# Last rows' operands in a gated unit: four buffers of parts, their stores on GpSimd's queue, and a step between the loads of raw blocks and their use

## The chip, the cores and the metric

The kernel runs on one core of a Trainium2 chip. A core has TensorE (PE, with its weight loads shown as PEld), VectorE (DVE), ScalarE (ACT), GpSimd (POOL) and SyncE (SP), each with its own queue of instructions that it takes strictly in order; they meet only at semaphores. DMAs are issued from the queues of SP and POOL. The metric is the device time of one execution in microseconds, the median of the runs shown; the clock is the one that TensorE was granted, as a share of full speed.

## The reference, cut to what matters

A transformer block with adaptive layer norm: attention with 32 heads, then a gated unit, on 2048 rows of 576 features. The part around the change is the gated unit:

```python
h = _layernorm(x, axis=-1) * (1 + cb) + sb
g = jnp.einsum("bsd,df->bsf", h, w_gate)      # 576 -> 4608
u = jnp.einsum("bsd,df->bsf", h, w_up)        # 576 -> 4608
h = _sigmoid(g) * u
x = x + gb * jnp.einsum("bsf,fd->bsd", h, w_down)   # 4608 -> 576
```

All in float32, to float32's precision.

## The kernel before

The kernel keeps float32's precision on a faster matmul type: each operand is a sum of a rounded part and a remainder, and a product takes the three larger of the four partial products. In the gated unit it also cuts the matrix products in two by two blocks and takes seven products in place of eight (Strassen's scheme in Winograd's form): seven operands made of sums and differences of blocks of the rows, seven of the weights.

The rows are handled in two halves of 1024. For a half, the unit goes over 18 blocks of 256 hidden features; in each it runs the seven products in the order 1, 6, 2, 7, 5, 4, 3 (`ORDER`). A product is 14 matmuls (line 1027): seven for the gate, seven for the up projection. Behind products 6 and 7 stands a down projection of the block before (`down`, line 1063): 48 matmuls into eight banks in turn, of which three exist (`d`), each emptied by an addition on DVE into `Oa` (line 1067). The second half of the rows runs the same blocks, and reads its weight operands back from HBM.

In the first half every weight operand `w` is made on the chip, three products ahead (`LOOK`), into one of four buffers: POOL builds the sums S1, S2, S3 of raw weight blocks (`put`, line 875), ACT rounds (line 909), DVE takes the remainder of five sixths of it and POOL that of the last sixth, 64 partitions of it (both line 914), and SP stores it for the second half (`ws`, line 915). A product's seventh matmul is the first that reads POOL's share. SP also loads the raw weight blocks (lines 850 and 852) and the down weights (line 1047).

Beside the first half's blocks runs a generator, `last_rows`, one step at every second product. It finishes the rows of the second half: their output projection, their layer norm, six transposed blocks for each 512 rows, stored as `hs`, and at its end their operands for the seven products. For the operands it goes three times (i = 0, 1, 2: three slices of features) through the following: load four raw blocks `B` from `hs` (line 1186), then `operand_parts`: seven parts, each a copy rounded on ACT into a buffer `ho` (line 713), a remainder on POOL (line 715; for i = 2 line 720, twice for 32 partitions), and a store of `ho` to `xs` (lines 716 and 721); between them four differences of the blocks on POOL (line 724). The raw blocks lie in five buffers `B`, the parts in `ho`. The stores are read only when the second half begins.

The order on each engine is set when the program is built. A scheduler places the instructions of all steps by its own costs, except on PE, whose order is as written from the ninth block on (`manual_schedule`). So a generator's step is where its instructions are handed over, not where they run.

Of the kernel before, what the change touches and what calls it, by code (L numbers as in the profile page):

```python
# [16 lines left out]
F32R = mybir.dt.float32r  # L17
# [6 lines left out]
P = 128  # L24
# [27 lines left out]
def tile_block(ctx, tc, x_in, wqkv, wo, w_gate, w_up, w_down, c_in, w_mod, out):  # L52
    nc = tc.nc
# [94 lines left out]
    def ln_stats(pool, xt, mv):  # L148
        st = pool.tile([P, 2, nc.vector.BN_STATS_DIM], F32, name="st", bufs=2)
        for g in range(2):  # L150
            nc.vector.bn_stats(st[:, g, :], xt[:, g, :] if len(xt.shape) == 3 else xt[:, g * HALF : (g + 1) * HALF])
        nc.vector.bn_aggr(mv, st)

    def ln_scales(pool, mv, rs):
        for _ in ln_scales_steps(pool, mv, rs):
            pass
# [522 lines left out]
    def ln_rows(z, t, x1, eng):  # L679

        zx = z[:, :, 0:HALF]
        eng.tensor_scalar(
            zx, x1, mv2[:, t, 0:1], rs2[:, t : t + 1], op0=ALU.subtract, op1=ALU.mult
        )
        nc.gpsimd.tensor_copy(
            z[:, :, HALF:384].rearrange("p g (r c) -> p g r c", c=32),
            z[:, :, HALF - 32 : HALF].unsqueeze(2).to_broadcast([P, 2, 3, 32]),
        )

    def ln_spill(zs, ch, psum, pool, put):  # L690


        for g in range(2):
            for i in range(3):
                pt = psum()
                for j, z in enumerate(zs):
                    nc.tensor.transpose(pt[:, j * P : (j + 1) * P], z[:, g, i * P : (i + 1) * P], ident)
                ev = pool.tile([P, 512], F32, name="ev", bufs=2)
                c = 3 * g + i
                put(ev, pt, mcol2[:, 0, c : c + 1], mcol2[:, 1, c : c + 1])  # L700
                nc.sync.dma_start(hs[g, i, :, ch * 512 : (ch + 1) * 512], ev)
                yield

    def operand_parts(half, i, blocks, parts, hi, lo_eng, queue):

        b11, b12, b21, b22, t3 = blocks

        def put(k, t):  # L710
            s = ORDER.index(k)
            ho = parts()
            hi(ho[:, 0, :], t)
            if i < 2:
                lo_eng.tensor_sub(ho[:, 1, :], t, ho[:, 0, :].bitcast(F32))
                queue.dma_start(xs[half, s, :, i : i + 4 : 3, :].bitcast(F32), ho.bitcast(F32))
            else:
                for q in (32, 96):
                    lo = ho[q : q + 32, 0, :]
                    lo_eng.tensor_sub(lo, t[q : q + 32], lo.bitcast(F32))  # L720
                queue.dma_start(xs[half, s, :, 2, :].bitcast(F32), ho[:, 0, :].bitcast(F32))

        def sub(to, a, b):
            nc.gpsimd.tensor_tensor(to, a, b, op=ALU.subtract)

        sub(t3, b22, b12)
        put(1, b11)
        yield
        sub(b12, b12, b11)
        put(3, b22)  # L730
        yield
        sub(b22, b22, b12)
        put(2, b21)
        yield
        sub(b21, b21, b22)
        for k, t in ((6, b22), (7, t3), (5, b12), (4, b21)):
            put(k, t)
            yield
# [335 lines left out]
    blocks = {(0, 0): begun}  # L1074
# [34 lines left out]
    def last_rows():  # L1109


        def psum():
            return pd.tile([P, 512], F32, name="d")

        with tc.tile_pool(name="fin", bufs=1, side="right") as pool:
            w = pool.tile([P, 2, 2, D], F32R, name="w")
            nc.gpsimd.dma_start(w, wod)
            for t0 in (0, 4):
                od = pool.tile([P, 4, 256], F32, name="od")
                nc.sync.dma_start(od[:, :, 0:192], oend[:, t0 : t0 + 4, :])  # L1120
                nc.sync.dma_start(od[:, :, 192:256], oend[:, t0 : t0 + 4, 128:192])
                yield
                pt = psum()
                for j in range(4):
                    nc.tensor.transpose(pt[:, j * P : (j + 1) * P], od[:, j, 0:P], ident)
                oh = pool.tile([P, 512], F32R, name="oh")
                ol = pool.tile([P, 512], F32R, name="ol")
                nc.vector.tensor_copy(oh, pt)
                nc.vector.tensor_sub(ol, pt, oh.bitcast(F32))
                pt = psum()  # L1130
                for j in range(4):
                    nc.tensor.transpose(pt[:, j * P : (j + 1) * P], od[:, j, P:256], ident)
                om = pool.tile([P, 512], F32R, name="om")
                omh = pool.tile([P, 512], F32R, name="omh")
                nc.vector.tensor_copy(om[0:64], pt[0:64])
                nc.vector.tensor_copy(omh[64:P], pt[64:P])
                nc.vector.tensor_sub(om[64:P], pt[64:P], omh[64:P].bitcast(F32))
                yield
                for j in range(4):
                    rows = slice(j * P, (j + 1) * P)  # L1140
                    xt = pool.tile([P, D], F32, name="xt", bufs=2)
                    nc.sync.dma_start(xt, x1p[:, t0 + j, :])
                    for h in range(2):
                        cols = slice(h * HALF, (h + 1) * HALF)
                        acc = psum()
                        ts_ = ((oh, 0, 0), (oh, 1, 0), (ol, 0, 0), (om, 0, 1), (om, 1, 1))
                        for n, (a, i, k) in enumerate(ts_):
                            nc.tensor.matmul(
                                acc[:, :HALF], a[:, rows], w[:, i, k, cols], start=n == 0, stop=n == 4
                            )  # L1150
                        nc.vector.tensor_add(xt[:, cols], xt[:, cols], acc[:, :HALF])
                    nc.sync.dma_start(x1d[:, t0 + j, :], xt)
                    yield

        def modulated(ev, pt, scale, bias):
            nc.scalar.activation(ev, pt, AF.Identity, scale=scale, bias=bias)

        with tc.tile_pool(name="zp2", bufs=1, side="right") as zp:
            for ch in (2, 3):
                zs = []  # L1160
                for t in range(4 * ch, 4 * ch + 4):
                    z = zp.tile([P, 2, 384], F32, name="z", bufs=4)
                    x1 = z[:, :, 0:HALF]
                    for g in range(2):
                        nc.sync.dma_start(z[:, g, 0:HALF], x1d[:, t - 8, g * HALF : (g + 1) * HALF])
                    ln_stats(zp, x1, mv2[:, t, :])
                    zs.append(z)
                four = slice(4 * ch, 4 * ch + 4)
                ln_scales(zp, mv2[:, four, :], rs2[:, four])
                for j, z in enumerate(zs):  # L1170
                    ln_rows(z, 4 * ch + j, z[:, :, 0:HALF], nc.vector)
                yield
                yield from ln_spill(zs, ch, psum, zp, modulated)
        with tc.tile_pool(name="xop2", bufs=2) as pool:

            def get():
                return [pool.tile([P, 512], F32, name="B", bufs=5) for _ in range(5)]

            def parts():
                return pool.tile([P, 2, 512], F32R, name="ho")  # L1180

            for i in range(3):
                blocks = get()
                for (g, r), t in zip(((0, 0), (0, 1), (1, 0), (1, 1)), blocks):
                    cols = slice(HW + r * 512, HW + (r + 1) * 512)
                    nc.sync.dma_start(t, hs[g, i, :, cols])
                yield from operand_parts(1, i, blocks, parts, nc.scalar.copy, nc.gpsimd, nc.sync)

    def banks(*names):
        return [pg.tile([P, 512], F32, name=n, bufs=3 if n == "x" else 1) for n in names]  # L1190
# [1 line left out]
    def half(t, v):  # L1192
        return t[:, 512 * v : 512 * (v + 1)]

    rows2 = last_rows()
    before = None
    for n, (hf, b, k) in enumerate(seq):
# [84 lines left out]
```

## Time and profile before

| | us |
|---|---|
| median of 3 runs | 2952.17 (2949.37 to 2953.37) |
| the profiled execution | 2953.87 |
| its span, from the first to the last instruction | 2952.1 |

| engine | busy us | share of the span |
|---|---|---|
| PE | 2890.3 | 98% |
| PEld | 1888.9 | 64% |
| DVE | 2139.3 | 72% |
| ACT | 1614.7 | 55% |
| POOL | 813.7 | 28% |

Where the last rows' operands run (ACT's first copy into `ho` of this stage starts at 1933.66 us, its last at 2064.34 us), the profile shows:

| | us |
|---|---|
| subtractions on POOL for the operands, lines 715, 720 and 724 | 18.4, 20.2, 16.6 |
| copies on ACT, line 713, 21 of them | 13.0 |
| idle time of ACT just before these copies | 60.2 |

How to read it: a line of the profile names an engine, an operation, its output and input by the program's names, and a count; a wait names the instruction that waited and the one that released it. A share of busy time is a mean over stages with different limits; what a stage is bound by is read from its own waits. The stage of the gated unit runs from about 1660 us to the end.

### The profile page before, as it was taken

How to read it: one execution, taken by the hardware profiler on the slowest of the kernel's cores; microseconds unless marked ns; L12 is line 12 of the kernel's file. 1: busy time of each engine (PE TensorE's matmuls, PEld its weight loads, DVE VectorE, ACT ScalarE, POOL GpSimd, SP SyncE). 2: the span in 40 equal slices, each digit the busy share in tenths (PEclk: the TensorE clock that was granted, in tenths of full speed). 3: DMA queues.
4: the chain of work that ended last, by engine and by line, in shares of the span. 5: the costliest groups of instructions: out<-in, count | busy, mean ns of one | idle time of the engine just before them, and what ended most of it. 6: DMA issues, size and time to landing. Idle time of an engine off the chain costs nothing.

```text
span 2952.1 us, 46641 instructions
## 1 busy us (share of the span) xinstructions
PE 2890.3 (98%) x17141; PEld 1888.9 (64%) x17141; DVE 2139.3 (72%) x3896; ACT 1614.7 (55%) x3022; POOL 813.7 (28%) x972
## 2 busy tenths in 40 slices
PE   7999999999999999999999999998999999999999
PEld 5756333433344444444443788877888888888888
DVE  7465888888888888998883777766777555555555
ACT  3214889999999888999889323333333111111111
POOL 3102005444303111464103534467544100000000
PEclk9999999999999999999999999999999999999999
DMA  5325213333302111222214766676666845444443
GB/s 178 101 87 185 71 31 131 121 130 126 117 26 80 53 33 44 90 75 70 60 62 161 271 237 235 232 265 237 217 215 217 317 161 178 166 166 170 162 157 136
DMA packets 137261, 425.97 MB, mean 144 GB/s; under 512 B 18884, under 2 KB 56520, under 8 KB 124744
## 3 DMA queue, kind: packets, MB, share of 16 engines
q1 hardware_dynamic: 121272, 342.42, 34.2%
q0 software_dynamic: 15760, 80.56, 7.6%
q8 instruction: 135, 2.21, 0.3%
q14 instruction: 94, 0.77, 0.1%
HBM read 264.45 MB, written 157.95 MB: 143 GB/s over the span
## 4 chain that ended last, share of the span: by engine, by line
PE 90%; ACT 2%; DVE 2%; DMA 2%; POOL 2%; issue 1%; SPq 1%; POOLq 0%; DVEq 0%; ACTq 0%
PE o L533 17%; PE d L1063 14%; PE x L1027 14%; PE s L955 13%; PE s L442 11%; PE bg L1027 5%; PE bu L1027 5%; PE s L294 4%; PE s L330 2%; PE s L672 2%; ACT p L959 1%; PE s L557 1%; ACT oT L547 1%; POOL S L875 0%; DMA B<-hs 0%
## 5 line engine op out<-in xcount | busy, mean ns | idle before, releaser
L959 ACT ACTIVATE p<-s 128x512 f32<-128x512 f32 x2048 | 1068.5, 608 | 142.9 <-PE s L442 91.7
L455 DVE TENSOR_REDUCE mx<-s 128x1 f32<-128x512 f32 x1568 | 1019.6, 686 | 169.7 <-PE s L442 156.2
L442 PE MATMUL s<-k,q 54*128 54x512 f32 x1920 | 649.7, 439 | 2.1 <-ACT p L959 1.6
L955 PE MATMUL s<-q,k 56*128 56x512 f32 x1920 | 578.7, 433 | 2.6
L955 PEld LDWEIGHTS s<-q,k 56*128 56x128 f32 x1920 | 274.8, 186 | 472.8 <-ACT p L959 304.7
L533 PE MATMUL o<-p,vaug 128*32 128x512 f32 x4096 | 555.8, 608 | 0.0
L1063 PE MATMUL d<-wd,hh 128*128 128x288 f32 x2304 | 470.0, 299 | 17.7 <-DVE Oa L1067 17.1
L1063 PEld LDWEIGHTS d<-wd,hh 128*128 128x128 f32 x2304 | 379.5, 191 | 26.9 <-DVE Oa L1067 21.5
L1067 DVE TENSOR_TENSOR Oa<-Oa,d 128x288 f32<-128x288 f32 x576 | 257.7, 452 | 152.6 <-PE d L1063 149.0
L442 PEld LDWEIGHTS s<-k,q 54*128 54x128 f32 x1920 | 308.4, 185 | 69.3 <-ACT p L959 38.5
L1063 PE MATMUL d<-wd,hl 128*128 128x288 f32 x1152 | 344.0, 299 | 0.0
L1027 PE MATMUL x<-k,w 128*128 128x512 f32 x994 | 239.6, 392 | 2.2 <-DVE u L1241 2.2
L1039 ACT ACTIVATE u<-u 128x512 f32<-128x512 f32 x72 | 45.5, 632 | 328.4 <-DVE u L1229 309.7
L1063 PEld LDWEIGHTS d<-wd,hl 128*128 128x128 f32 x1152 | 219.9, 191 | 0.3 <-DVE hl L1043 0.3
L1027 PEld LDWEIGHTS x<-k,w 128*128 128x128 f32 x994 | 184.7, 188 | 39.6 <-DVE u L1241 2.9
L533 PEld LDWEIGHTS o<-p,vaug 128*32 128x32 f32 x4096 | 83.5, 108 | 164.9 <-issue 149.4
L1069 POOL DMA_DIRECT2D out_dram<-Oa x16 | 8.7, 542 | 607.5 <-DVE Oa L1067 607.5
L1036 ACT ACTIVATE sg<-x 128x512 f32<-128x512 f32 x36 | 21.5, 598 | 282.5 <-PE x L1027 282.5
L450 DVE CUSTOM_DVE_ANT_0 rise<-s,rise 128x512 f32<-128x512 f32 x240 | 163.5, 681 | 0.0
L448 ACT ACTIVATE rise<-s 128x512 f32<-128x512 f32 x240 | 151.4, 631 | 0.0
L914 POOL TENSOR_TENSOR w<-S,w 64x256 fp32r<-64x256 f32 x69 | 72.0, 1044 | 214.2 <-ACT w L909 202.5
L1027 PE MATMUL x<-w,w 128*128 128x512 f32 x504 | 121.3, 390 | 0.0
(240 smaller groups left out, 3812.8 us busy)
## 6 DMA issues: line engine op xcount, KB each, us to landing
w<-ws SPq DMA_DIRECT2D x126, 640.0 KB
ws<-w SPq DMA_DIRECT2D x124, 640.0 KB
wd<-wds SPq DMA_DIRECT2D x36, 1152.0 KB
wds<-w POOLq DMA_DIRECT2D x18, 1152.0 KB, 4.5
k<-kd SPq DMA_DIRECT2D x30, 360.0 KB
w<-in_B_w_down_dram POOLq DMA_DIRECT2D x18, 576.0 KB, 5.0
q<-qd SPq DMA_DIRECT2D x64, 144.0 KB
raw<-in_B_w_gate_dram SPq DMA_DIRECT2D x34, 256.0 KB
```

The source lines that it names most:

```text
L294: nc.tensor.matmul(acc, w, hT[:, t, cols], start=n == 0, stop=n == len(ts_) - 1)
L442: nc.tensor.matmul(sp, qs[rows, qt * P : (qt + 1) * P], ks[rows, kc * 512 : (kc + 1) * 512], start=True, stop=True,)
L448: nc.scalar.activation(rise, sp, AF.Relu)
L450: nc.vector.tensor_tensor_reduce(rise, sp, rise, 1.0, -3.0e38, ALU.add, ALU.max, mx[0][:, qt, 0:1])
L455: nc.vector.tensor_reduce(mx[h][:, qt, j : j + 1], sp, axis=AX.X, op=ALU.max)
L533: nc.tensor.matmul(acc[32 * j : 32 * j + 32, :], vaug[:, kt, (2 * p + h) * VW : (2 * p + h) * VW + 32], probs[2 * c + h], start=kt == 0, s ...
L914: eng.tensor_sub(w[rows, :, to, :], src[rows, :, a, :], w[rows, :, a, :].bitcast(F32))
L955: nc.tensor.matmul(sT, ks[rows, kcols], qs[rows, c * 512 : (c + 1) * 512], start=True, stop=True)
L959: state["exp"] = nc.scalar.activation(pr, sT, AF.Exp, scale=SCALE)
L1027: nc.tensor.matmul(acc[v], w[:, v, a, :], X[s][:, b, :], start=first and n == 0, stop=n == 6, skip_group_check=not first,)
L1063: nc.tensor.matmul(acc[:, :HALF], a[:, f, rows], w[:, f, cols], start=n == 0, stop=n == 5)
L1067: nc.vector.tensor_add(Oa[:, t, cols], Oa[:, t, cols], acc[:, :HALF])
```

## The change

The parts get a pool of four buffers instead of two; the generator takes a step between the loads of raw blocks and the first part made of them; and the stores of the parts are issued from POOL's queue instead of SP's.

```diff
             def parts():
-                return pool.tile([P, 2, 512], F32R, name="ho")
+                return pool.tile([P, 2, 512], F32R, name="ho", bufs=4)
 
             for i in range(3):
                 blocks = get()
                 for (g, r), t in zip(((0, 0), (0, 1), (1, 0), (1, 1)), blocks):
                     cols = slice(HW + r * 512, HW + (r + 1) * 512)
                     nc.sync.dma_start(t, hs[g, i, :, cols])
-                yield from operand_parts(1, i, blocks, parts, nc.scalar.copy, nc.gpsimd, nc.sync)
+                yield
+                yield from operand_parts(1, i, blocks, parts, nc.scalar.copy, nc.gpsimd, nc.gpsimd)
```

No instruction of PE moves. ACT, POOL and SP get another order from the point on at which the operands begin. On POOL, before the change, from the third set's first part to POOL's share of the weights for the second product of the fourth block with operands, `w<-S_24925` (`w<-` are POOL's shares of weight operands, `ho<-B` remainders of parts, `B<-B` differences of blocks):

```order
L720 TENSOR_TENSOR ho<-B,ho 32x512 x2
L914 TENSOR_TENSOR w<-S_24576,w 64x2x128
L875 TENSOR_TENSOR S_24925<-S_24924,raw_24585 128x384 x2
L724 TENSOR_TENSOR B<-B 128x512
L914 TENSOR_TENSOR w<-raw_24585,w 64x2x128
L724 TENSOR_TENSOR B<-B 128x512
L720 TENSOR_TENSOR ho<-B,ho 32x512 x2
L724 TENSOR_TENSOR B<-B 128x512
L720 TENSOR_TENSOR ho<-B,ho 32x512 x2
L724 TENSOR_TENSOR B<-B 128x512
L914 TENSOR_TENSOR w<-S_24925,w 64x2x128
```

And with the change, the last rows ahead of POOL's share of the weights for the second product of that third block, `w<-S_24572`:

```order
L914 TENSOR_TENSOR w<-raw_24236,w 64x2x128
L721 DMA xs<-ho 128x512
L724 TENSOR_TENSOR B<-B 128x512
L720 TENSOR_TENSOR ho<-B,ho 32x512 x3
L721 DMA xs<-ho 128x512
L720 TENSOR_TENSOR ho<-B,ho 32x512 x2
L721 DMA xs<-ho 128x512
L720 TENSOR_TENSOR ho<-B,ho 32x512 x2
L721 DMA xs<-ho 128x512
L720 TENSOR_TENSOR ho<-B,ho 32x512
L721 DMA xs<-ho 128x512
L914 TENSOR_TENSOR w<-S_24572,w 64x2x128
```

All parts of the third set and all 21 stores now stand ahead of this weight operand of the third block; before, the same row of the fourth block still had four of the third set's parts behind it.

On SP, with the change, the third set's second, third and fourth raw blocks (`B<-hs`; `raw` are weight blocks, `ws` stores of weight operands):

```order
L1186 DMA B<-hs 128x512
L915 DMA ws<-w 128x1280
L1186 DMA B<-hs 128x512
L915 DMA ws<-w 128x1280
L850 DMA raw_24643<-in_B_w_gate_dram 128x2x256
L852 DMA raw_24643<-in_B_w_gate_dram 128x1x256
L850 DMA raw_24643<-in_B_w_up_dram 128x2x256
L852 DMA raw_24643<-in_B_w_up_dram 128x1x256
L1186 DMA B<-hs 128x512
L915 DMA ws<-w 128x1280 x2
```

Before the change these three loads stood together in one row, behind a store of a part:

```order
L716 DMA xs<-ho 128x2x512
L1186 DMA B<-hs 128x512 x3
L915 DMA ws<-w 128x1280
L721 DMA xs<-ho 128x512
L915 DMA ws<-w 128x1280
```

The stores of parts have left SP's queue, and between the loads of a set now stand stores and loads of the weights.

## The prediction

> **What bounds the kernel now.** I read the busy line first, then the waits of the gated unit, then TensorE block by block around the last rows' operands, and at last the queues of ACT and POOL there. PE is busy for 98% of the span (the page's first part), so only its gaps can be won or lost. In the gated unit a block of the hidden dimension is seven products and two down projections, and its first product is the one that reads `X[0]`. Cut at these first products (us, then the busy time of PE, PEld, DVE, ACT and POOL, the granted clock, the DMA share and GB/s), the blocks on and behind the last rows' operands stand thus:
>
> ```profile
> 1924.90:1966.50 41.60, 38.22 (x198) 33.82 (x197) 24.78 (x41) 15.28 (x24) 29.51 (x25) 0.92 0.79 272
> 1966.50:2008.40 41.90, 37.26 (x196) 32.70 (x195) 26.40 (x42) 13.95 (x22) 27.88 (x25) 0.96 0.71 236
> 2008.40:2051.40 43.00, 38.26 (x195) 33.91 (x194) 26.36 (x40) 14.76 (x23) 30.11 (x26) 0.92 0.78 270
> 2051.40:2092.80 41.40, 37.44 (x196) 32.26 (x195) 31.32 (x44) 14.07 (x22) 31.35 (x27) 0.96 0.60 218
> 2092.80:2127.80 35.00, 35.00 (x196) 31.11 (x195) 25.70 (x42) 11.42 (x18) 16.90 (x16) 1.00 0.63 217
> ```
>
> I call the first three blocks A, B and C. An undisturbed block takes 35.00 us, so the four blocks with operands lose 41.60 + 41.90 + 43.00 + 41.40 - 4 x 35.00 = **27.9 us**. That is all the change can win; POOL's busy time in them (28 to 31 us, against 16.9) is what it can run into. Who waits for whom there (1925 to 2080 us: total, times, longest):
>
> ```profile
> ACT ho L713 <- DMA xs<-ho: 35.9, 11, 7.2
> ACT ho L713 <- DMA B<-hs: 18.6, 5, 6.5
> PE d L1063 <- DVE Oa L1067: 14.4, 5, 4.7
> DVE w L914 <- ACT w L909: 8.3, 7, 5.0
> PE x L1027 <- DVE u L1241: 2.2, 1, 2.2
> ```
>
> One of the stalls, engine by engine (start, duration, instruction, idle time before it and its releaser):
>
> ```profile
> 1989.84 0.62 ACT L713 CAST ho<-B 128x512 fp32r<-128x512 f32 x1 [5.21 <-DMA B<-hs]
> 1992.60 1.02 DVE L914 TENSOR_TENSOR w<-raw,w 128x512 fp32r<-128x512 f32 x1 [4.97 <-ACT w L909]
> 1994.04 0.63 PE L1063 MATMUL d<-wd,hh 128*128 128x288 f32 x2 [4.51 <-DVE Oa L1067]
> ```
>
> ACT stands at a cast of an operand, the weights' cast stands behind it on ACT, the weights' remainder waits on DVE, the additions that empty PE's banks stand behind that, and PE stops. PE idles 14.4 + 2.2 = 16.6 us in this way; the other 11 us of the 27.9 are matmuls at a lower granted clock behind each stop (0.92 and 0.96 above). The price of one stop shows in one product, whose halves stand ahead of a stop and behind it:
>
> ```profile
> 2051.42 1.75 PE L1027 MATMUL x<-k,w 128*128 128x512 f32 x7
> 2055.34 3.02 PE L1027 MATMUL x<-k,w 128*128 128x512 f32 x7 [2.17 <-DVE u L1241]
> ```
>
> That is 1.3 us for seven matmuls and some 2 us until the clock is back.
>
> **The change part by part.** *Four buffers of parts* end waits of ACT for a store two parts earlier, 35.9 us of ACT's time. *Stores on POOL's queue* take 21 issues off SP, each 0.43 us in the median, and put them on POOL (min/median/max in ns, as POOL issues the same tiles for the first rows):
>
> ```profile
> L716 SPq DMA_DIRECT2D xs<-ho x14: 370/426/1247, 1937.0 to 2028.8; - x14
> L716 POOL DMA_DIRECT2D xs<-ho x5: 725/725/792, 1229.0 to 1301.9; - x5
> L721 POOL DMA_DIRECT2D xs<-t x5: 540/560/631, 1323.6 to 1359.2; - x5
> 1238.90 0.72 POOL L716 DMA_DIRECT2D xs<-ho  x1 [0.30 <-POOL ho L715]
> ```
>
> 14 x 0.73 + 7 x 0.56 = 14.1 us, and 0.30 more where the store stands right behind the subtraction that fills it. SP computes nothing; POOL makes a sixth of every weight operand and the sums S1 to S3. (The Trainium skill, "DMA: Bandwidth & Descriptors", section "Issuing engines are not separate DMA queues", says that transfers from all queues share the same 16 DMA engines and that another issuing engine saves only sequencer time; by that the stores land no sooner and the saving is SP's 9 us, which PE waits for in no row above. It speaks against this part and leaves the sum as it is.)
>
> *Blocks a turn ahead.* The order shows the first set's loads where they were, so the wait of 4 us for them stays. Those of the second and third sets come earlier in SP's queue, but into buffers that POOL still reads.
>
> *What the new order does* outweighs all three. The fences of the section on the change show it: nothing holds the parts back on ACT, so the order now packs all 21 into blocks A and B, where they were spread over four. POOL runs strictly in this order, and between the weights of A's sixth product and those of C's second (`w<-S_24572`) now stand 40 operand subtractions, 21 DMA issues, 10 sums and, with that last one, 10 weight operands. The price of each (busy us, mean ns, 1925 to 2080 us):
>
> ```profile
> L720 POOL TENSOR_TENSOR ho<-B,ho 32x512 fp32r<-32x512 f32 x14 | 20.2, 1444 | 1.6 <-ACT ho L713 0.7
> L715 POOL TENSOR_TENSOR ho<-B,ho 128x512 fp32r<-128x512 f32 x14 | 18.4, 1317 | 14.1 <-ACT ho L713 13.8
> L724 POOL TENSOR_TENSOR B<-B 128x512 f32<-128x512 f32 x12 | 16.6, 1380 | 7.5 <-DMA B<-hs 6.8
> L914 POOL TENSOR_TENSOR w<-S,w 64x256 fp32r<-64x256 f32 x15 | 15.0, 999 | 12.1 <-issue 7.1 <-ACT w L909 3.8 <-POOL ho L715 0.5
> L914 POOL TENSOR_TENSOR w<-raw,w 64x256 fp32r<-64x256 f32 x11 | 9.4, 857 | 0.9
> L875 POOL TENSOR_TENSOR S<-raw 128x384 f32<-128x384 f32 x8 | 10.0, 1268 | 2.9 <-DVE w L914 2.8
> L875 POOL TENSOR_TENSOR S<-raw,raw 128x384 f32<-128x384 f32 x8 | 9.1, 1153 | 0.3
> ```
>
> Subtractions 20.2 + 18.4 + 16.6 = 55.2; weights 10 x 0.94 (24.4 over 26) = 9.4; sums 10 x 1.2 (between the two rows) = 12.0; issues 14.1: **90.7 us of work in one queue.** It starts and is due here:
>
> ```profile
> 1935.72 1.29 POOL L715 TENSOR_TENSOR ho<-B,ho 128x512 fp32r<-128x512 f32 x1
> 1938.38 2.66 POOL L724 TENSOR_TENSOR B<-B 128x512 f32<-128x512 f32 x2 [1.37 <-DMA B<-hs]
> 1924.90 3.47 PE L1027 MATMUL x<-k,w 128*128 128x512 f32 x14
> 1928.21 1.75 PE L1027 MATMUL bg<-k,w 128*128 128x512 f32 x7
> ```
>
> The queue is done no earlier than 1935.7 + 90.7 = 2026.4. To this come its waits: 0.3 for the first loads (most of the 1.37 is now filled by the first issue), 0.3 at each of four stores right behind their subtraction (1.2), about 2 for A's fifth product, whose end frees a weight buffer, with DVE's remainder behind it, and about 4 for the third set's fourth block. That block's load stands on SP behind a load that waits for POOL's last part of the second set, then a store, a load, a store and four raw loads: some 4 us of issue, and then the landing:
>
> ```profile
> 1975.97 0.42 SPq L1186 DMA_DIRECT2D B<-hs  x1
> 1980.45 0.62 ACT L713 CAST ho<-B 128x512 fp32r<-128x512 f32 x1 [6.52 <-DMA B<-hs]
> ```
>
> 4.5 us here; so 8.5 or more, while POOL has two stores, two subtractions and a third store left, 5 us. Together 7.5: **2033.9**. Undisturbed, PE is at C's second product at 1924.9 + 2 x 35.0 + 3.3 = 1998.2, and at its seventh matmul, the first that reads POOL's part of the weights, 1.4 us later, 1999.6. So blocks A to C lose 2033.9 - 1999.6 = 34.3 us, and the slow clock behind this last stop 2 more: 36.3. Behind it POOL has two sums and one weight instruction until the next product that could wait, with a down projection between, and no operands are left, so I count nothing further. The net is 36.3 - 27.9 = **+8.4 us**. The ACT path ends near the same point: four casts stand ahead of the sigmoid of B's `u3` and wait for POOL's last subtractions, so it adds little on top.
>
> The two ends: with the operand subtractions at 1.28, weights at 0.86, sums at 1.15 and no waits, 51.2 + 8.6 + 11.5 + 14.1 = 85.4, done at 2021.1, a loss of 21.5, or -6.4 us net. That is a floor, since the order is fixed. At the other end POOL and DVE slow each other when both work without a break:
>
> ```profile
> 2041.72 2.63 POOL L720 TENSOR_TENSOR ho<-B,ho 32x512 fp32r<-32x512 f32 x2
> 2055.35 6.89 POOL L720 TENSOR_TENSOR ho<-B,ho 32x512 fp32r<-32x512 f32 x4
> 2057.60 1.78 DVE L914 TENSOR_TENSOR w<-S,w 128x512 fp32r<-128x512 f32 x1
> ```
>
> 1.72 us each instead of 1.32. With 40 at 1.72 the queue has 68.8 instead of 55.2, +13.6, or +22 net. (The Trainium skill's "GPSIMD Engine Reference", section "1. Specifications", says that POOL shares its SBUF interfaces with VectorE, in contention above all with instructions of two SBUF inputs, as this weight remainder is; a fuller POOL queue would then meet more of them, towards the upper end. The trace agrees as far as 6.89 us for four.)
>
> **The rivals.** *POOL bound, but with no more loss than now* (no change): its work runs near the floor with few waits, 25 to 30 us lost, 2949 to 2956 us. For it speaks that DVE idles while PE stands, which makes POOL quicker; against it the four named waits. *The stores were the fault* (faster): only the stops that follow an ACT wait for a store go away, about half of the 27.9, so 2952.2 - 14 = 2938 us. For it speak the 35.9 us of ACT; it decides only if POOL's queue reaches C's second weights some 14 us after 1999.6, while the floor is 2021.1. *Contention* (slower still): the 22 us above, 2974 us. *The loads are not ahead* where it matters: true of the first set, and part of my sum; were the third set's wait of 4 us gone, 2956.6.
>
> **How the numbers follow.** The profiled execution took 2953.87 us with a span of 2952.1, 1.7 above the median of the runs; from the median 2952.17 + 8.4 = **2960.6 us**. Chances: POOL's queue as summed 0.60, contention 0.12, POOL near its floor 0.19, stores at fault 0.09. A measurement here tells 0.2% (5.9 us, so above 2958.1 or below 2946.3) from no change. Nearly all of contention and most of the forecast's spread (2954 to 2970) lie above: slower 0.65; the rest of the forecast and most of the floor within: 0.25; faster 0.10. The range goes from the floor's 2946 to the contended end's 2974.
>
> **What would show it.** Right: the parts' casts and POOL's subtractions end near 2035 instead of 2074; POOL is over 90% busy from 1940 to 2034; C's second product waits for POOL (or PE stops just ahead of it for `u` at line 1242); blocks A to C lose about 36 us, and the next ones nothing. Wrong: PE's waits in these blocks fall below 10 us; POOL has gaps of several us; a part's store on POOL takes well off 0.73 us; or time goes in blocks without operands.

## The result, and the profile after

The changed kernel takes 2968.49 us in the median of 4 runs (2967.64 to 2974.47), the kernel before on the same chip 2952.77 us: a ratio of **1.0059 (95% interval 1.0041 to 1.0076)**, 15.7 us between the medians (whose own ratio is 1.0053). The direction, the place and the packing of the parts as the cause held; the last stop came over ACT and not from POOL's queue, and the forecast size, +8.4 us, was about half.

The same cut of the trace as before, at the first products of the blocks A, B, C and the next one (kernel after; columns as in the prediction: us, busy time of PE, PEld, DVE, ACT and POOL, granted clock, DMA share, GB/s):

```profile
1921.70:1963.80 42.10, 37.42 (x197) 33.29 (x196) 25.72 (x41) 15.96 (x25) 36.37 (x34) 0.92 0.82 291
1963.80:2028.20 64.40, 43.93 (x195) 38.39 (x194) 26.30 (x37) 16.65 (x28) 49.70 (x46) 0.79 0.55 196
2028.20:2069.90 41.70, 36.88 (x196) 32.22 (x196) 33.17 (x47) 13.12 (x20) 28.15 (x27) 0.96 0.68 236
2069.90:2104.90 35.00, 35.00 (x196) 31.11 (x195) 25.76 (x42) 11.44 (x18) 16.95 (x16) 1.00 0.62 211
```

A, B and C lose 42.10 + 64.40 + 41.70 - 3 x 35.00 = **43.2 us**, the fourth block nothing. Before, four blocks lost 27.9. The difference is 15.3 us, about the whole result. POOL's work has moved from four blocks into two and a half: 36 us busy in A and 50 in B, where it had 28 to 31. B holds most of the loss, at a granted clock of 0.79.

Who waits for whom (after, 1925 to 2080 us: total, times, longest):

```profile
PE d L1063 <- DVE Oa L1067: 22.9, 4, 9.2
ACT ho L713 <- DMA B<-hs: 22.4, 4, 9.8
ACT ho L713 <- POOL B L724: 21.8, 4, 9.2
POOL B L724 <- DMA B<-hs: 13.5, 2, 7.2
ACT ho L713 <- DMA xs<-ho: 6.8, 2, 5.5
PE x L1027 <- DVE u L1242: 4.8, 1, 4.8
```

ACT's wait for stores did go, from 35.9 us to 6.8. In its place ACT waits for POOL's differences (line 724; 0.7 us in the same stretch before) and for raw blocks. One stop from its cause to PE, in block B (after, the timelines of SP, ACT, DVE and PE; start, duration, idle time before and its releaser in brackets):

```profile
1995.65 0.67 SPq L1186 DMA_DIRECT2D B<-hs  x1
2005.90 0.62 ACT L713 CAST ho<-B 128x512 fp32r<-128x512 f32 x1 [9.83 <-DMA B<-hs]
2006.43 0.83 ACT L909 CAST w<-S 128x768 fp32r<-128x768 f32 x1
2007.34 1.70 DVE L914 TENSOR_TENSOR w<-S,w 128x512 fp32r<-128x512 f32 x1 [9.52 <-ACT w L909]
2011.73 0.85 PE L1063 MATMUL d<-wd,hh 128*128 128x288 f32 x2 [9.16 <-DVE Oa L1067]
```

The third set's fourth raw block comes 10.2 us after its issue. ACT stands at the cast that reads it, the weights' cast behind it is late, DVE stands at the weights' remainder, the additions that empty `d` stand behind that, and PE stops for 9.16 us: the chain of the kernel before, with a longer wait at its head. And the place where the prediction said that POOL's queue would decide (after, timelines of ACT, DVE, PE and POOL):

```profile
2025.38 0.62 ACT L713 CAST ho<-B 128x512 fp32r<-128x512 f32 x1 [5.49 <-DMA xs<-ho]
2034.08 0.68 DVE L1242 TENSOR_TENSOR u<-x,u 128x512 f32<-128x512 f32 x1
2034.82 3.36 PE L1027 MATMUL x<-k,w 128*128 128x512 f32 x7 [4.83 <-DVE u L1242]
2036.38 0.73 POOL L914 TENSOR_TENSOR w<-S,w 64x256 fp32r<-64x256 f32 x1
2037.97 1.85 PE L1027 MATMUL bg<-k,w 128*128 128x512 f32 x7
```

POOL ends the weights of C's second product at 2037.1. That product's seventh matmul, the first that reads them, runs about 1.4 us behind the product's start of 2037.97, at 2039.4. So POOL's queue was in time by 2.3 us, and the path over ACT, DVE and `u` was the one PE waited for.

### The profile page after: what moved, and what is told of

It reads as the page before. It is cut to its first block, busy times and chain, and to the rows that moved or that the text cites. A ratio compares the mean times of both kernels' runs of the same rounds, so it can differ in the third digit from the quotient of the medians.

```text
span 2965.9 us, 46646 instructions
## 1 busy us (share of the span) xinstructions
PE 2890.3 (97%) x17141; PEld 1890.9 (64%) x17141; DVE 2141.4 (72%) x3896; ACT 1613.8 (54%) x3022; POOL 826.0 (28%) x993
## 4 chain that ended last, share of the span: by engine, by line
PE 90%; ACT 2%; POOL 2%; DMA 2%; DVE 2%; issue 1%; SPq 0%; POOLq 0%; DVEq 0%; ACTq 0%
PE o L533 17%; PE d L1063 14%; PE x L1027 14%; PE s L955 13%; PE s L442 11%; PE bg L1027 5%; PE bu L1027 5%; PE s L294 4%; PE s L330 2%; PE s L672 2%; ACT p L959 1%; DMA B<-hs 1%; PE s L557 1%; ACT oT L547 1%; POOL B L724 0%
## 5 line engine op out<-in xcount | busy, mean ns | idle before, releaser
L1063 PE MATMUL d<-wd,hh 128*128 128x288 f32 x2304 | 471.6, 299 | 27.9 <-DVE Oa L1067 26.6
```

Of the source, the lines that this page charges most:

```text
L1063: nc.tensor.matmul(acc[:, :HALF], a[:, f, rows], w[:, f, cols], start=n == 0, stop=n == 5)
```

## The experiments

Each kernel is compared with the kernel before on its own chip. "Loss" is what the blocks from A on take beyond 35.00 us each, in one profiled execution; they are counted until no block loses more, and an undisturbed block more or less leaves the loss as it is. How far it varies from one execution to the next was not measured. Line numbers behind an added line are shifted by it.

| kernel | ratio to before (95% interval) | blocks, us | loss, us |
|---|---|---|---|
| before | 1 | 4, 167.9 | 27.9 |
| after | 1.0059 (1.0041 to 1.0076) | 3, 148.2 | 43.2 |
| e1_bufs | 1.0002 (0.9992 to 1.0011) | 4, 169.9 | 29.9 |
| e2_queue | 1.0089 (1.0072 to 1.0106) | 3, 158.0 | 53.0 |
| e3_yield | 0.9994 (0.9984 to 1.0003) | 4, 166.6 | 26.6 |
| f_h4 | 1.0015 (1.0005 to 1.0024) | 4, 173.3 | 33.3 |
| q_h3b9 | 1.0039 (1.0026 to 1.0052) | 3, 141.0 | 36.0 |
| z1_after | 1.0054 (1.0039 to 1.0069) | 3, 144.8 | 39.8 |
| p_after | 0.9953 (0.9939 to 0.9968) | 8, 293.1 | 13.1 |
| p_before | 0.9958 (0.9942 to 0.9975) | 8, 295.3 | 15.3 |
| zp_after | 0.9941 (0.9927 to 0.9954) | 8, 290.0 | 10.0 |
| p3_q | 0.9966 (0.9953 to 0.9978) | 10, 366.6 | 16.6 |
| zp3_q | 0.9955 (0.9942 to 0.9967) | 10, 362.9 | 12.9 |
| nolo_p | 0.9922 (0.9907 to 0.9937) | 8, 282.1 | 2.1 |

### The three edits, one at a time

Four buffers alone:

```diff
-                return pool.tile([P, 2, 512], F32R, name="ho")
+                return pool.tile([P, 2, 512], F32R, name="ho", bufs=4)
```

> Four buffers of parts alone; the stores stay on SP and no step is added. Theory (the stores on POOL's queue let the order pack all parts into two and a half blocks, and the loss is in that edit): the operands still run through four blocks, ACT's waits for stores fall from 36 us to under 15, PE's waits fall a little, 2940 to 2954 us, most likely 2947. Rival (four buffers are what lets the parts pack, so that ACT stands at casts for POOL's results): at least half of the change's loss shows here, 2959 us or more. Rival of the prediction (the stores were the fault of the old loss): 2938 us.

No change: 1.0002, neither the small gain of the theory nor the loss of its rival. The waits of e1_bufs from 1915 to 2105 us:

```profile
ACT ho L713 <- POOL B L724: 20.1, 3, 7.9
ACT ho L713 <- DMA B<-hs: 18.9, 5, 5.6
ACT ho L713 <- DMA xs<-ho: 5.5, 1, 5.5
```

ACT's wait for stores is almost gone and nothing is gained. ACT arrives sooner at a cast whose block POOL has not made yet. The stores were the last of several waits at the same casts, not their cause.

The queue of the stores alone, with two buffers:

```diff
-                yield from operand_parts(1, i, blocks, parts, nc.scalar.copy, nc.gpsimd, nc.sync)
+                yield from operand_parts(1, i, blocks, parts, nc.scalar.copy, nc.gpsimd, nc.gpsimd)
```

> The stores on POOL's queue alone, with two buffers of parts and no added step. Theory (this edit alone packs the parts; two buffers only add waits for stores): the last part ends within about 115 us of the first as with the change, 2962 to 2980 us, most likely 2970. Rival (the four buffers pack the parts): 2950 to 2957 us, operands over four blocks.

2982.13 us against 2955.32, the slowest kernel of all and 2 us above the theory's range. The waits of e2_queue from 1915 to 2105 us:

```profile
ACT ho L713 <- DMA xs<-ho: 59.6, 14, 8.4
PE d L1063 <- DVE Oa L1067: 24.1, 3, 10.0
PE x L1027 <- DVE u L1241: 17.5, 2, 13.4
```

In the order of POOL's instructions, this edit alone takes the number of its weight remainders between the first part and the last from 20 to 9; with four buffers alone it is 18, and after the whole change 9. So the queue edit packs the parts and costs 53.0 - 27.9 = 25 us; why the scheduler then places them so was not looked into. At two buffers ACT's waits for stores grow to 59.6 us, and the whole change, with four buffers and the added step, wins 53.0 - 43.2 = 10 us of it back. The step alone changes nothing (below), so this is most likely the buffers, but no run has them with the queue and without the step.

The step alone:

```diff
+                yield
                 yield from operand_parts(1, i, blocks, parts, nc.scalar.copy, nc.gpsimd, nc.sync)
```

> The added step between loads and parts alone. Theory (the step moves nothing that matters, since the scheduler places by its own costs and the loads wait for buffers that POOL still reads): within 3 us of the kernel before, 2950 to 2956 us, and ACT's waits for the raw blocks' loads stay near 18 us. Rival (loads a turn ahead end these waits): they fall to under 8 us and the time by 4 to 8 us, 2945 to 2949.

0.9994: no difference that can be measured. ACT's waits for raw blocks stay at 19.3 us from 1915 to 2105 us (18.6 in the kernel before).

### Taking ACT out of the chain

Four buffers, the stores on SP, and the rounding of the parts on POOL instead of ACT:

```diff
-                yield from operand_parts(1, i, blocks, parts, nc.scalar.copy, nc.gpsimd, nc.sync)
+                yield from operand_parts(1, i, blocks, parts, nc.gpsimd.tensor_copy, nc.gpsimd, nc.sync)
```

> Four buffers, stores on SP, no added step, and the parts are rounded on POOL instead of ACT (21 copies of 0.61 us more on POOL, ACT never stands at a part). Theory (PE stops because ACT, and behind it DVE, stand at casts of parts that wait; POOL by itself has three products of lead): PE's waits in the blocks with operands fall from 16.6 us to under 8, 2930 to 2943 us, most likely 2937. Rival (POOL's own queue is the bound wherever parts stand close together; up to 15 of its instructions for parts in a row are 17 us against three products' 10 to 16): 2950 to 2962 us, with PE or ACT waiting for POOL's shares of weights.

A ratio of 1.0015, in the rival's range. The waits of f_h4 from 1915 to 2105 us:

```profile
PE bg L1027 <- POOL w L914: 19.0, 2, 13.9
POOL B L724 <- DMA B<-hs: 14.6, 2, 9.2
```

ACT no longer stands at parts, PE's stops at the down projections shrink to 2.7 us, and PE waits for POOL's share of the weights instead, with POOL's own wait for a raw block inside it. Here the bound that the prediction named appears in the open: whichever engine holds the parts in a row holds up the weights that stand behind them in its queue.

### What the loads and POOL's amount are worth after the change

Nine raw blocks instead of five, three buffers of parts instead of four, otherwise the kernel after:

```diff
-                return [pool.tile([P, 512], F32, name="B", bufs=5) for _ in range(5)]
+                return [pool.tile([P, 512], F32, name="B", bufs=9) for _ in range(5)]
...
-                return pool.tile([P, 2, 512], F32R, name="ho", bufs=4)
+                return pool.tile([P, 2, 512], F32R, name="ho", bufs=3)
```

> The kernel after the change with three buffers of parts instead of four and nine raw blocks instead of five, so that four loads of the next set need not wait for POOL's last parts of the set before. The order on POOL is as packed as after (9 weight differences among the parts). Theory (of the 43.1 us lost, the 13.5 us in which POOL waits for the fourth block of a set are a part of the path): POOL's wait for loads goes to 0 to 3 us, its parts end about 11 us sooner, ratio to the kernel before 1.002 (0.999 to 1.004). Rival (the order of ACT and DVE behind the packed parts sets the loss, whatever the loads do): the second set is packed closer still, and the ratio stays at 1.005 to 1.008.

The added step is left out as well. The ratio is 1.0039, at the upper end of the theory's range; its interval overlaps that of the change. The loss falls from 43.2 to 36.0 us. The waits of q_h3b9 from 1915 to 2105 us:

```profile
ACT ho L713 <- DMA xs<-ho: 43.8, 13, 7.0
POOL B L724 <- DMA B<-hs: 0.6, 1, 0.6
```

POOL's wait for loads is gone (13.5 to 0.6), but with three buffers ACT's wait for stores is back, so the two can't be parted here: 7 us is the net of both, and what the loads alone are worth is not shown.

The kernel after with 7 of POOL's 40 operand subtractions fewer (the low by low term of the last 64 columns is left out):

```diff
-                for q in (32, 96):
+                for q in (32,) if half else (32, 96):
...
                     modulate(row, mods, HALVES, [(mcol2[:, 0, :], 1.0), (gb_b, None)])
+                    for c in (2, 5):
+                        nc.vector.memset(mcol2[96:P, :, c], 0.0)
```

> The kernel after the change with one of the two 32-row differences of each part of the third set left out (7 fewer POOL instructions of 1.39 us, 9.7 us). Rows 96 to 127 of the third operand are made zero for it, so that the products hold high by high, low by high and high by low; the low by low term of these 64 columns is left out. Theory (POOL's work between its weights is what is waited for): the third set's parts end about 9.7 us sooner and the time falls by 4 to 10 us, ratio to the kernel before 1.0035 (1.002 to 1.0045). Rival (load waits and ACT's order set the loss): the wait for the third set's fourth block fills again or the loss in block B, ahead of this set, stays all there is; no more than 2 us, ratio 1.005 to 1.007.

1.0054: the theory's gain of 4 to 10 us did not come in the times; the profiled blocks lose 39.8 us, 3.4 less. So 9.7 us of POOL's work from the third set, taken from the end of the row, were worth about a third of themselves in the trace and nothing measurable in the times. The stop of 4.8 us ahead of `u` is gone, but PE's waits for the additions into `Oa` are 29.0 us where they were 22.9. That these stops, ahead of the third set's end, are set by the loads and by ACT's place in the row is argued from the waits above and not tried.

### The same work, spread

The rounding of each part is tied to the last matmul of the product just written, so that the scheduler can't place a part earlier than one to every second product. In the kernel after (p_after) and in the kernel before (p_before, with its two buffers and SP's queue):

```diff
+    latest = {}
+
+    def kept_back(does):
+        return lambda *a, **kw: tied(does(*a, **kw))
+
+    def tied(step):
+        tc.add_manual_dep(
+            step.ins, latest["mm"].ins.name,
+            mybir.DependencyInfo(mybir.DependencyClass.Sync, mybir.DependencyReason.DATA),
+            reason="a part to every second product",
+        )
...
-                nc.tensor.matmul(
+                latest["mm"] = nc.tensor.matmul(
...
-                yield from operand_parts(1, i, blocks, parts, nc.scalar.copy, nc.gpsimd, nc.gpsimd)
+                yield from operand_parts(1, i, blocks, parts, kept_back(nc.scalar.copy), nc.gpsimd, nc.gpsimd)
```

> The kernel after the change, and the rounding of each of the 21 parts tied to the last matmul of the product that the program has just written, so that no part can be set earlier than one to every second product (6 blocks of 7 products instead of 2.5). Work and stores on POOL are those of the kernel after the change, and POOL has 46 weight differences between the first and the last part instead of 9. Theory (the packing of the parts costs the time, not their amount): the 43.1 us lost in the blocks A to C go almost entirely, 0 to 10 us remain, ratio to the kernel before 0.990 (0.987 to 0.995). Rival (the amount of POOL's work, 14 us of it store issues): each block of 35 us now holds 3.5 parts, about 11 us, beside some 16 us of POOL's weights; if POOL's amount is what costs, the blocks stay longer than 35 us, the loss is spread over six blocks but stays near 30 to 43 us, ratio 1.002 to 1.006.

> The kernel before the change with the same tie and nothing else: the stores stay on SP's queue, two buffers of parts. 39 weight differences of POOL between the first and the last part instead of 20. Theory (packing): its 27.9 us go to 0 to 8 us, ratio 0.991 (0.989 to 0.995), and p_after is no more than 3 us from it, since a store of 0.73 us to every second product is hidden. Rival (stores or two buffers at fault): ACT's roundings still wait for stores on SP's queue, 10 us or more of the loss stay, and p_after with four buffers and POOL's queue is faster by that much.

Both are faster than the kernel before, by 0.5% and 0.4%, and equal to each other, though the gain is about half of what the theory forecast. The eight blocks with parts in p_after, then in p_before:

```profile
1922.65:2215.78 293.13, 285.12 (x1555) 248.96 (x1554) 220.49 (x328) 102.22 (x158) 199.20 (x181) 1.00 0.71 244
```

```profile
1918.10:2213.36 295.26, 286.50 (x1556) 249.09 (x1554) 221.32 (x328) 102.24 (x158) 191.59 (x160) 1.00 0.70 242
```

The loss is 13.1 and 15.3 us, at a clock of 1.00. All of POOL's work is still there in p_after, its 14.1 us of store issues too. This tells packing from amount: of the 43.2 us, 30 were due to where the parts stood. And with the parts spread, the queue of the stores and the number of buffers make no difference that can be measured, so the 35.9 us of ACT's waits for stores in the kernel before were a sign of the packing as well: in the blocks of p_before, with the same queue and two buffers, ACT waits for no store.

### What is left of the loss

p_after still loses 13.1 us. Three kernels ask why: the 7 fewer instructions of z1_after in it (zp_after), one part to every third product (p3_q), both (zp3_q; p3_q and zp3_q are without the added step).

```diff
-        if n >= 5 and n % 2:
+        if n >= 5 and (n % 2 if n < 57 else n % 3 == 0):
```

> p_after (the kernel after the change, each part tied to every second product) and the third set's parts without their second 32-row difference (7 POOL instructions of 1.39 us fewer, rows 96 to 127 of that operand zero, the low by low term of 64 columns left out). In p_after the two blocks with the third set's parts are the longest left, 39.9 and 37.2 us, and there DVE's same 42 instructions take 30.6 and 28.7 us busy against 25.7 us in a block without parts. Theory (what is left is DVE slowed by POOL's work beside it, and POOL at 30 of 40 us): those two blocks fall to 36 to 37.5 us and the time by 3 to 6 us, ratio to the kernel before 0.9940 (0.9925 to 0.9950). Rival (what is left is the tie itself or ACT's waits for products): no change, 0.9945 to 0.9965.

> The kernel after the change without its added step, each part tied as in p_after, and from product 57 on one part to every third product instead of every second (9 blocks instead of 6). Theory (each part costs a share of DVE's and POOL's time only where it makes a block's work too dense): 14 us lost in p_after fall to 4 to 9 us, since no block then has more than 2.3 parts, ratio 0.993 (0.9915 to 0.995). Rival (every part costs the same small stop, 0.5 to 0.7 us, wherever it is set): the same 14 us over nine blocks, ratio 0.994 to 0.997.

> Both at once: one part to every third product and the third set's second differences left out (low by low of 64 columns left out as in zp_after). Theory: 2 to 5 us of loss remain, ratio 0.992 (0.9905 to 0.994), the shortest of all. Rival (each part costs a fixed stop): ratio 0.994 to 0.9965.

With fewer instructions on POOL the loss falls to 10.0 us, while the ratio, 0.9941, can't be told from p_after's 0.9953. Spreading the parts wider does not help (0.9966, loss 16.6), and both together do no better (0.9955, 12.9). So the rest does not come from the density of the work: a part costs 13.1/21 = 0.6 us in p_after and 16.6/21 = 0.8 us in p3_q, as the rival had it. The last run takes POOL's remainders of the parts out of p_after and leaves ACT's casts, the stores and line 724 (the rounded part is stored in the remainder's place, so the second half's products lack the remainders):

```diff
+            if half and i < 2:
+                twice = ho[:, 0:1, :].bitcast(F32).to_broadcast([P, 2, 512])
+                queue.dma_start(xs[half, s, :, i : i + 4 : 3, :].bitcast(F32), twice)
-            if i < 2:
+            elif i < 2:
...
-                for q in (32, 96):
+                for q in () if half else (32, 96):
```

> p_after (the kernel after the change, each part tied to every second product) without POOL's remainders of the parts: the 28 instructions of lines 715 and 720 (42.9 us of POOL in p_after) are left out and the rounded part is stored in the remainder's place, so the second half's products lack them. ACT's 21 casts, POOL's 21 stores of the same size and the 12 differences of line 724 (15.5 us) stay. p_after loses 13.9 us in the blocks with parts, 0.66 us to a part, and p3_q lost 17.6 us with the same parts spread wider. Theory (POOL's work beside DVE makes DVE's weight remainders slow, 1.18 us each against 0.94 without parts, and their lateness is what PE still waits for): the loss goes with POOL's work, 13.9 x 15.5/58.4 = 4 us left, DVE's mean near 1.0 us, ratio to the kernel before 0.992 (0.990 to 0.9935). Rival (ACT's cast of 0.62 us ahead of the weights' cast is the stop): 11 to 14 us stay, ratio 0.9945 to 0.9965.

(The losses of 13.9 and 17.6 us in this expectation are 13.1 and 16.6 when the blocks are cut at their first products, as in the table.) The loss goes to 2.1 us and the ratio to 0.9922, as the theory had it. Its eight blocks, and its only wait of PE in them:

```profile
1925.82:2207.96 282.14, 281.29 (x1555) 249.18 (x1554) 205.78 (x328) 102.54 (x158) 162.41 (x153) 1.00 0.73 254
```

```profile
PE d L1078 <- DVE Oa L1082: 0.8, 2, 0.7
```

In p_after PE waits ten times as long:

```profile
PE d L1075 <- DVE Oa L1079: 4.8, 6, 1.4
PE x L1039 <- DVE u L1254: 3.0, 5, 1.4
```

The same 328 instructions of DVE take 220.5 us in p_after and 205.8 us here. DVE's weight remainders (count, busy us, mean ns), in p_after, in nolo_p, and in five blocks of the kernel before without parts:

```profile
L914 DVE TENSOR_TENSOR w<-S,w 128x512 fp32r<-128x512 f32 x32 | 37.9, 1183 | 5.5 <-ACT w L909 3.9 <-PE d L1075 1.0 <-DMA ws<-w 0.3
L914 DVE TENSOR_TENSOR w<-raw,w 128x512 fp32r<-128x512 f32 x24 | 27.9, 1161 | 0.4
```

```profile
L917 DVE TENSOR_TENSOR w<-S,w 128x512 fp32r<-128x512 f32 x32 | 31.7, 991 | 6.4 <-ACT w L912 5.8 <-DMA ws<-w 0.6
L917 DVE TENSOR_TENSOR w<-raw,w 128x512 fp32r<-128x512 f32 x24 | 24.0, 999 | 0.8
```

```profile
L914 DVE TENSOR_TENSOR w<-S,w 128x512 fp32r<-128x512 f32 x20 | 19.7, 984 | 4.0 <-ACT w L909 4.0
L914 DVE TENSOR_TENSOR w<-raw,w 128x512 fp32r<-128x512 f32 x16 | 15.3, 957 | 0.0
```

The instructions of DVE that read a bank of PE's results did not change (`Oa<-Oa,d` took 449 ns in p_after and 450 in nolo_p), while `u<-u` went from 1030 to 712 ns. It is shown that POOL's remainders cause the rest of the loss, and that DVE's instructions beside them are longer. That this lengthening is the whole path from the one to the other is argued from the waits of PE, all of which are for DVE.

zp_after has the lowest ratio of the kernels that still make every part, 0.59% under the kernel before (0.46% to 0.73%); p_after, which leaves no term out, is 0.47% under it.

## Why the prediction was right in its direction and short in its size

**What the change can win, 27.9 us now.** It stood, but as a bound of something else: p_after and p_before show that about half of it goes when the parts are spread, while the edits at the buffers and the step win none of it.

**The new order outweighs the rest.** Right, and the runs name the edit: the stores' queue alone packs the parts and costs 25 us. The rival *the stores were the fault* fell with e1_bufs, in which ACT waits for one store (5.5 us) and the time stays.

**POOL's queue, 90.7 us of work.** The groups of POOL from its first remainder to the weights of C's second product (after, 1932.5 to 2037.1 us):

```profile
L720 POOL TENSOR_TENSOR ho<-B,ho 32x512 fp32r<-32x512 f32 x14 | 19.5, 1390 | 1.0
L715 POOL TENSOR_TENSOR ho<-B,ho 128x512 fp32r<-128x512 f32 x14 | 18.2, 1314 | 0.3
L724 POOL TENSOR_TENSOR B<-B 128x512 f32<-128x512 f32 x12 | 15.8, 1319 | 13.9 <-DMA B<-hs 13.5
L716 POOL DMA_DIRECT2D xs<-ho x14 | 10.2, 731 | 0.6 <-POOL ho L715 0.6
L721 POOL DMA_DIRECT2D xs<-ho x7 | 3.9, 563 | 0.6 <-POOL ho L720 0.6
```

Subtractions 53.5 (55.2 predicted), issues 14.1 (14.1), weights and sums 20.0 (21.4): 87.6 us, 3 less than summed. The contended end, 1.72 us for a subtraction, did not come: 1.31 to 1.39.

**Its waits, 7.5 us: the term that failed.** The queue took 104.6 us, so 17 us lay between its instructions, of which 13.5 are waits for the fourth raw blocks of the second and the third set. The prediction had 4 for the third set and none for the second. The second set's (after, timelines of SP and POOL):

```profile
1955.71 0.68 SPq L1047 DMA_DIRECT2D wd<-wds  x1
1956.48 0.94 SPq L1186 DMA_DIRECT2D B<-hs  x1
1970.14 2.63 POOL L724 TENSOR_TENSOR B<-B 128x512 f32<-128x512 f32 x2 [7.25 <-DMA B<-hs]
```

The prediction took 4.5 us from issue to landing, from a load of the kernel before that stood behind one store of weights (640 KB). It saw the four raw loads in SP's queue and counted their issues, not what they move. A nearer row stood in the same trace: three raw blocks issued from 1981.74 us on, right behind four raw loads, were used at 1989.90, 8.2 us later. Here the second set's 256 KB come 13.6 us after the issue, behind four loads of raw weights and the down weights, 2 MB; the third set's, also behind four raw loads, come after 10.2.

The loads ahead are not all of it. POOL's stores now run on a DMA queue of their own (9.18 MB, which is all 21 of them), and while the second set's block was on its way the DMA engines moved 2.76 MB of SP's queue and 1.59 MB of POOL's; for the third set's it was 0.99 and 1.44 MB. So the stores that the change moved to POOL are a likely part of the delay, which no run tries by itself. Nor are bytes the whole: in the third set's wait the DMA share is 1.00 for the first 5.0 us and 0.30 for the rest, and why the block took that long then is open.

The queue's end was to come 98.2 us behind its start and came at 104.6, 6.4 us of the 7 that are missing. That it was so near is partly luck: the work was 3 us shorter than summed, and the waits 9.5 longer.

**PE waits for POOL at C's second product.** By POOL alone the loss would be 2037.1 less the due time, 1999.6 - 3.2 (this trace begins the blocks 3.2 us sooner): 40.7 us, to 34.3 predicted. The ACT path, said to end near the same point, ended 2.3 us later and set the 43.2; the prediction's 2 us for the slow clock behind the last stop are about as much. The prediction named that last stop, ahead of `u`, but not the two long stops in B's down projections, 8.0 and 9.2 us; B alone loses 29.4 of the 43.2 us.

**What would show it.** Right: POOL's last subtraction ends at 2035.5 (forecast near 2035; in a trace whose blocks begin 3.2 us sooner), PE stops ahead of `u`, the next block loses nothing, a store on POOL takes 0.73 us. Wrong: POOL was busy 76.7 of the 94 us from 1940 to 2034, 82% and not over 90%, with two gaps of 6 to 7 us; that was set down as a sign against the forecast, and it marks the term that failed.

**Contention.** The prediction gave it 0.12 as a cause of a longer POOL queue. In this kernel the queue did not grow by it. What the spread kernels show is the other side: DVE's instructions are longer beside POOL's remainders, and without these remainders 13.1 - 2.1 = 11 us of loss go, over 21 parts. (POOL's own took 1.57 and 1.49 us in p_after.)

## What to carry to other kernels

A wait that heads the list on an engine that is not the bound may be one of several at the same instruction; before paying to end it, ask what the instruction would wait for next. Where a scheduler places side work, a change of queue or buffers can move all of it: compare the orders, and if the side work must not hold up the main one, tie it to the main work's progress, which here won more than any of the buffers. A small load can wait for what is issued ahead of it and for what other queues move in the same time: look for a row with the same loads ahead of it, and count their bytes and not only their issues.

## What the runs showed of the hardware that was not expected

A store of 512 KB that POOL issues lands later beside the gated unit than beside the first rows' work. From issue to landing (line 716, kernel after, 1925 to 2050 us, then 1200 to 1310 us):

```profile
DMA to landing us min/median/max: 3.4/6.1/9.1
```

```profile
DMA to landing us min/median/max: 3.2/3.3/8.5
```

This fits the cost of two buffers with POOL's queue, and the one cast that still waited 5.5 us for a store with four; why the landing is later was not tried. (In the two stretches the DMA engines moved 232 and 108 GB/s.)

DVE's 328 instructions took 14.7 us more beside 42.9 us of POOL's remainders, 0.34 us for each us of POOL, and the price did not fall when the same work was spread over more blocks: the ten blocks of p3_q took 274.6 us of DVE, 17 more than ten undisturbed ones at 25.7 us. (The Trainium skill, "GPSIMD Engine Reference", section "1. Specifications", has POOL share its SBUF interfaces with VectorE, in contention with DVE instructions of two SBUF inputs; the weight remainders are of that kind, and their 1.18 us against 0.99 us agree with it.)
